# Summing the two parts of the cosines on TensorE, spacing the gate's steps, and moving second-layer parts in each stage's last unit

## The chip, the core and the metric

The kernel runs on one NeuronCore of a Trainium2 chip. The core has TensorE (PE) for matrix products, VectorE (DVE), ScalarE (ACT) and GpSimd (POOL) for work on elements, and SyncE (SP), which issues the transfers. The metric is the device time of one execution in microseconds. Before the change three executions took 1617.32, 1617.62 and 1620.14 us, so the median is 1617.62 us.

## What is computed

Three layers follow one another. The first is clustered attention: a query sees only the keys whose nearest centroid is the same as its own. The nearest centroid is the argmax of 16 cosines per row, so small errors there would change the mask. Then come a layer with softplus and a mixture whose gate is normalised eight times over rows and columns (Sinkhorn).

```python
q_assign = np.argmax(np.einsum('bhsd,hcd->bhsc', q_n, c_n), axis=-1)
k_assign = np.argmax(np.einsum('bhsd,hcd->bhsc', k_n, c_n), axis=-1)
mask = q_assign[:, :, :, None] == k_assign[:, :, None, :]
scores = np.where(mask, scale * np.matmul(q, k.transpose(0, 1, 3, 2)), -1e9)
attn = softmax(scores); x = attn @ v          # 2 x 8 heads, 768 rows, 64 wide
g = softplus(x @ w_in); x = g @ w_out         # 1536 x 512, hidden 2048
P = np.exp(x @ w_gate - max)                  # 8 experts
for _ in range(8):
    P /= P.sum(1, keepdims=True) + 1e-09
    P /= P.sum(0, keepdims=True) + 1e-09
    P *= N / E
out = sum(P[:, e:e+1] * (np.maximum(x @ w1[e], 0) @ w2[e]) for e in range(8))
```

## The kernel before, in words

**Two-part numbers.** TensorE takes float32 operands in a short format. So each operand X is split into a high part (a cast) and a low part (X minus the cast), and a product is a sum of two to four matmuls over parts.

**Attention** works on 8 pairs of heads, `g` = 0 to 7. For each pair there is preparation (loads, splits, norms, cosines, argmax, one-hot rows) and then 4 half passes of scores, exponentials, transposes and products with V. The order is written out by hand: each step is an event with a place in time (`at`, and `sched_pair`, L505 to L543); the events are sorted and issued in that order, and pair `g+1` is prepared while pair `g` is attended. The compile step may still move an instruction forward on its engine where its own model finds the engine free. Categories named in `KEEP` (L665) are pinned behind what was issued before them on their engine.

The cosines of a pair are made in two halves of 384 rows (`hf`). `pair_sims` (L428) issues four matmuls for a half: two sources (q and k) times two parts of the source, and the stationary matrix `Z` holds the centroids' high and low parts side by side. So the 128 output rows are source x head x centroid part x 16 centroids, and the two centroid parts land in different rows. ACT copies the result to `sT`. `pair_simsT` (L446) transposes it back in three TensorE transposes into the PSUM tile `tp`, ACT copies the low-part columns to `s2`, and DVE adds high-part columns and `s2` into `A`. `pair_argmax` (L459) works on `A`. The PSUM tiles `sm` and `tp` share three buffers (tag `t`) with the transposes of the exponentials (`e_trans`, L597).

**The two later layers** are one list of units (L40): 8 + 8 units of the softplus layer (kind 1, halves `sb` 0 and 1 of the rows) and 32 + 32 of the mixture (kind 2). The first 8 form their products plainly (`plain_group`, L750); the others use seven groups of matmuls per unit (`group`, L695), six matmuls of 384 columns each. Groups 1 and 3 share the PSUM bank `lb` and wait for its evacuation. A unit's second layer is cut into four parts (`layer2`, L808), which are issued between the groups of the next unit, after groups 1, 3, 5 and 6 (L989). In a stage's last unit (`final`, L965; there are four) they are not: there the inputs of the next stage are split (`x_split`, L97 and L99) after each group, and after the last group come the four parts of the unit before and the four parts of this unit.

**The gate** needs the whole softplus output. `gate(b, hf)` (L863) makes the logits of half a batch entry: four float32 matmuls into PSUM, an ACT copy `ls`, three transposes and a DVE copy into `lt`. For `b` = 0 it is called after units 2 and 3 of the second stage (L993), in the bank `lb`. For `b` = 1 it is called in the first mixture unit. The first five mixture units are held (`hold`, L950): their activations wait in `late` until the gate is done. During them a queue of 22 steps is worked off, one after each group, four in the first unit and five in each later one (L951 to L960): two gates, two steps of `gate_max` (L878), 16 steps of `sinkhorn` (L892; step 0 works on rows on DVE and leaves column sums `cs`, step 1 sums them over partitions on TensorE in `cp`, L905, and scales), then `load_p` and `spread_p`. After the fifth unit all late activations run (L1007).

Of the kernel before, what the change touches and what calls it, by code (L numbers as in the profile page):

```python
# [7 lines left out]
F32 = mybir.dt.float32  # L8
F32R = mybir.dt.float32r
# [11 lines left out]
def attention_moe_moe2(ctx, tc, q, k, v, qt, kt, centroids, w_in, w_out, w_gate, w1, w2, eye, out, dbg=None):  # L21
# [265 lines left out]
    def prep_z(c2):  # L287
        for i in range(2):
            pc = ps_m.tile([P, P], F32R, tag="t", name=f"pc{i}")
            nc.tensor.transpose(pc, c2[:, i].rearrange("p a d -> p (a d)"), idr)  # L290
            pv = pc.bitcast(F32).rearrange("p (h j c) -> p h j c", j=2, c=NC_)
            nc.vector.tensor_copy(Z0[:, :, 96 + 16 * i : 112 + 16 * i], pv[:, 0])
            for j in range(2):
                js, o = slice(j * D, (j + 1) * D), 64 + 32 * j + 16 * i
                nc.vector.tensor_copy(Z[js, :, o : o + NC_], pv[js, :, j])

# [131 lines left out]
    def pair_sims(st, hf, ph):  # L428
        g = st.g
        if ph == 0:  # L430
            if hf == 0:
                st.sT = pp.tile([P, 2, CB], F32, tag="sT", name=f"sT{g}", bufs=1)
                st.A = pp.tile([P, 2, HT * 4, NC_], F32, tag="A", name=f"A{g}", bufs=1)
            st.sm = ps_m.tile([P, CB], F32, tag="t", name=f"sm{g}{hf}")
            for n in range(4):
                w, x = divmod(n, 2)
                if g:
                    c, m = Z[:, st.hp, 64 - 64 * w : 192 - 64 * w], st.HL[w][:, x]
                else:
                    o = 64 * w + 32 * x  # L440
                    c, m = Z0[:, x, 96 - o : 224 - o], st.AT[w, x]
                nc.tensor.matmul(st.sm, c, m[:, hf * CB : (hf + 1) * CB], start=n == 0, stop=n == 3)
        else:
            nc.scalar.copy(st.sT[:, hf], st.sm)

    def pair_simsT(st, hf, ph):  # L446
        g = st.g
        if ph == 0:
            st.tp = ps_m.tile([P, HT * 4, 2, NC_], F32, tag="t", name=f"tp{g}{hf}")
            tpv = st.tp.rearrange("p (t x) a c -> p t (x a c)", t=HT)  # L450
# [54 lines left out]
    def sched_pair(g, b0):  # L505
# [26 lines left out]
        for hf in range(2):  # L532
            P_(b0 + hf + 8.27, "sm", pair_sims, hf, 0)
            P_(b0 + hf + 8.27 + .1, "smc", pair_sims, hf, 1)
            P_(b0 + 2 * hf + 11.5, "tp", pair_simsT, hf, 0)
            P_(b0 + 2 * hf + 11.5 + .1, "tpc", pair_simsT, hf, 1)
            P_(b0 + 2 * hf + 11.5 + 0.65, "tpa", pair_simsT, hf, 2)
# [127 lines left out]
    KEEP = {'sp2': 1, 'fr': 0, 'sq': 1, 'red': 1, 'av': 1, 'am3': 1, 'tpa': 1, 'smc': 0, 'm0': 1, 'nw': 0, 'nv': 1, 'rw': 1, 'pz': 1, 'e1': 1, 'ln': 0}  # L665
# [194 lines left out]
    def gtile(shape, tag, b, nm):  # L860
        return ps_y.tile(shape, F32, tag=tag, name=nm) if b else ps_l.tile(shape, F32, tag="lb", name=nm)

    def gate(b, hf):  # L863
        lg = gtile([E, CB], f"y{hf}", b, f"lg{b}{hf}")
        for c in range(KC):
            nc.tensor.matmul(
                lg, wg[:, c, :], xt[b][:, c, hf * CB : (hf + 1) * CB], start=c == 0, stop=c == KC - 1
            )
        ls = mp.tile([E, CB], F32, tag="ls", name=f"ls{b}{hf}", bufs=2)
        nc.scalar.copy(ls, lg)  # L870
        tp = gtile([P, HT, E], "y4", b, f"lgT{b}{hf}")
        for t in range(HT):
            nc.tensor.transpose(tp[:, t, :], ls[:, t * P : (t + 1) * P], idf[:E, :E])
        nc.vector.tensor_copy(lt[:, b * NT + hf * HT : b * NT + (hf + 1) * HT, :], tp)

    sm = mp.tile([P, 2], F32, tag="gm", name="gm", bufs=1)

# [59 lines left out]
    def run(*steps):  # L937
        for l in steps:
            for fn in l:
                fn()  # L940

    run(*split_unit(units[0]))
    pend = []
    starts = [n for n in range(len(units)) if n == 0 or units[n - 1][:2] != units[n][:2]]
    for n, u in enumerate(units):
# [2 lines left out]
            return  # L948
        held = n - len(m1)
        hold = 0 <= held < NHOLD  # L950
        extra = []  # L951
        if hold:
            if held == 0:
                queue = [lambda hf=hf: gate(1, hf) for hf in range(2)]
                queue += [lambda ph=ph: gate_max(ph) for ph in range(2)]
                queue += [lambda it=it, ph=ph: sinkhorn(it, ph) for it in range(8) for ph in range(2)]
                queue += [lambda: load_p(0, 0), spread_p]
            k = 4 if held == 0 else 5
            extra, queue = queue[:k], queue[k:]
        if kind == 2 and fc == 0 and not hold:  # L960
            load_p(sb, e)
        if n + 2 in starts:
# [11 lines left out]
        for i in range(7):  # L974
            if not is_plain(u):
                group(u, i)
            elif i % 2 == 0:
                plain_group(u, i // 2)
            run(steps.get(i, []))
            if n + 1 in starts:  # L980
                key = f"{units[n + 1][0]}_{units[n + 1][1]}"
                if not is_plain(u):
                    x_split(key, sums, i)
                else:
                    for c in ((4,), (5,), (0, 1), (), (), (), (2, 3, 6))[i]:
                        x_split(key, sums, c)
            if extra:
                extra.pop(0)()
            if (i % 2 == 1 or i == 6) and pend and not hold and not final:  # L989
                layer2(pend[0], i // 2)  # L990
        for fn in extra:
            fn()
        if kind == 1 and sb == 1 and 2 <= fc < 4:  # L993
            gate(0, fc - 2)
        if pend and not hold:
            p_ = pend.pop(0)
            if final:
                for part in range(4):
                    layer2(p_, part)
        pend.append(u)  # L1000
        if final:
# [1 line left out]
            for part in (0, 2, 1, 3):  # L1003
                layer2(p_, part)
        if hold and held == NHOLD - 1:
            run(queue)
            for lu, q, cols in late:  # L1007
                if (0, lu[2]) not in PB:
                    load_p(0, lu[2])
                g = GF[lu, q][:, cols]  # L1010
                nc.vector.scalar_tensor_tensor(g, g, 0.0, PB[0, lu[2]][:, cols], ALU.max, ALU.mult)
                act_split(lu, q, cols)
# [39 lines left out]
```

## Time and profile before

| | us |
|---|---|
| executions without the profiler, median of 3 | 1617.62 |
| the profiled execution, its own time | 1615.32 |
| span of its trace, first to last instruction | 1613.5 |
| PE busy (matmuls) in the span | 1536.4 (95%) |
| DVE busy | 1079.2 (67%) |
| ACT busy | 851.7 (53%) |
| POOL busy | 687.2 (43%) |

Read it from the top: the trace covers the profiled execution except for 1.8 us around it. PE's busy time is an average over stages with different limits, and matmuls overlap in the pipeline, so 95% does not say that PE is the limit everywhere. In the profile's slices DVE is at nine tenths over the first sixth of the span, which is attention, and at five to six tenths in the mixture.

### The profile page before, as it was taken

The numbers are of one execution on the slowest core, as the hardware profiler recorded it, in microseconds if no ns is written. First come the engines' busy times: TensorE is split into PE (matmuls) and PEld (weight loads), VectorE is DVE, ScalarE is ACT, GpSimd is POOL, SyncE is SP. The second block draws the span as 40 slices with busy tenths as digits, with TensorE's granted clock in tenths as the row PEclk, the third lists the DMA queues.
The fourth block names the chain that finished last, engine by engine and source line by source line (L and its number), as shares of the span: only waits on it lengthen the run. The fifth ranks groups of instructions, "written<-read, shape, count | busy, mean of one in ns | idle before, by whom it ended". The sixth has DMA issues, their size and how long they took to land.

```text
span 1613.5 us, 22747 instructions
## 1 busy us (share of the span) xinstructions
PE 1536.4 (95%) x8134; PEld 1381.5 (86%) x8134; DVE 1079.2 (67%) x1772; ACT 851.7 (53%) x1727; POOL 687.2 (43%) x681
## 2 busy tenths in 40 slices
PE   5899999888999989999999999999999999999999
PEld 4788888787897868899999999988999999999997
DVE  5999999998554768665655656577655556565553
ACT  5888988766676754343434434344434434344342
POOL 4444533334755743434434443345333343343430
PEclk8999999999999999999999999999999999999999
DMA  7666620364211221222323223223223232232211
GB/s 218 179 168 167 177 65 7 124 219 143 78 58 53 59 60 54 84 60 83 75 66 89 62 79 74 77 66 115 64 77 86 58 86 65 76 78 73 79 53 46
DMA packets 135971, 145.18 MB, mean 90 GB/s; under 512 B 9169, under 2 KB 100785, under 8 KB 135857
## 3 DMA queue, kind: packets, MB, share of 16 engines
q1 hardware_dynamic: 135712, 143.66, 31.4%
q8 instruction: 64, 1.05, 0.3%
q14 instruction: 51, 0.41, 0.1%
q10 hardware_dynamic: 144, 0.07, 0.0%
HBM read 113.23 MB, written 11.58 MB: 77 GB/s over the span
## 4 chain that ended last, share of the span: by engine, by line
PE 64%; DVE 7%; ACT 4%; issue 1%; POOL 1%; DMA 0%; DVEq 0%; ACTq 0%; POOLq 0%
PE Y L842 32%; PE la L714 16%; PE mb L714 8%; PE lb L714 4%; PE y L823 2%; DVE gf L790 1%; DVE gl L804 1%; DVE wl L226 1%; ACT gh L803 1%; ACT u L788 1%; ACT u L787 1%; PE p L767 1%; ACT u L789 1%; DVE xS L75 0%; ACT wh L225 0%
## 5 line engine op out<-in xcount | busy, mean ns | idle before, releaser
L803 ACT CAST gh<-gf 128x384 fp32r<-128x384 f32 x316 | 161.5, 513 | 479.2 <-DVE gf L797 434.5
L214 POOL TENSOR_TENSOR wf<-wf 128x256 f32<-128x256 f32 x288 | 237.3, 846 | 346.9 <-DMA wf<-in_moe_w_dram 273.7
L232 POOL TENSOR_TENSOR w2l<-w2f,w2h 128x512 fp32r<-128x512 f32 x160 | 240.3, 1522 | 314.4 <-ACT w2h L231 314.4
L842 PE MATMUL Y<-w2h,gh 128*128 128x512 f32 x768 | 299.0, 389 | 0.7 <-ACT gh L803 0.7
L842 PE MATMUL Y<-w2l,gh 128*128 128x512 f32 x768 | 298.8, 389 | 0.0
L842 PE MATMUL Y<-w2h,gl 128*128 128x512 f32 x768 | 298.5, 389 | 0.0
L804 DVE TENSOR_TENSOR gl<-gf,gh 128x384 fp32r<-128x384 f32 x316 | 207.2, 659 | 96.1 <-ACT gh L803 89.4
L741 DVE TENSOR_TENSOR gf<-la,c 128x384 f32<-128x384 f32 x71 | 39.5, 557 | 254.2 <-PE la L714 254.0
L225 ACT CAST wh<-wf 128x512 fp32r<-128x512 f32 (+1 forms) x232 | 153.0, 684 | 35.1 <-PE la L714 24.8
L842 PEld LDWEIGHTS Y<-w2h,gl 128*128 128x128 f32 x768 | 144.1, 188 | 30.1
L842 PEld LDWEIGHTS Y<-w2h,gh 128*128 128x128 f32 x768 | 144.0, 188 | 22.3 <-ACT gh L803 1.2
L842 PEld LDWEIGHTS Y<-w2l,gh 128*128 128x128 f32 x768 | 144.2, 188 | 21.0
L797 DVE SCALAR_TENSOR_TENSOR gf<-gf,pb 128x384 f32<-128x384 f32 x177 | 151.1, 854 | 4.0
L226 DVE TENSOR_TENSOR wl<-wf,wh 128x512 fp32r<-128x512 f32 (+1 forms) x194 | 151.9, 809 | 1.0 <-ACT wh L225 0.9
L608 DVE TENSOR_TENSOR el<-t,eh 128x384 fp32r<-128x384 f32 x192 | 101.5, 544 | 11.8 <-ACT eh L604 10.6
L601 PE MATMUL t<-idf,E 128*128 128x128 f32 x576 | 96.4, 276 | 8.3 <-DVE el L608 5.0
L714 PE MATMUL mb<-chS,wh 128*128 128x384 f32 x288 | 98.2, 341 | 4.3 <-DVE gf L737 4.0
L604 ACT CAST eh<-t 128x384 fp32r<-128x384 f32 x192 | 91.6, 481 | 19.3 <-PE t L601 11.6
L231 ACT CAST w2h<-w2f 128x512 fp32r<-128x512 f32 x160 | 92.3, 618 | 16.7 <-PE y L823 8.7
L714 PE MATMUL la<-chA,wh 128*128 128x384 f32 x288 | 97.8, 340 | 1.6 <-DVE gf L797 1.6
L569 DVE TENSOR_REDUCE sc<-s 128x1 f32<-128x768 f32 x96 | 91.1, 949 | 12.0 <-PE s L561 11.4
L733 ACT COPY c<-la 128x384 f32<-128x384 f32 x144 | 68.8, 478 | 57.2 <-PE la L714 55.9
(210 smaller groups left out, 3478.0 us busy)
## 6 DMA issues: line engine op xcount, KB each, us to landing
w2f<-in_moe_w_dram SPq DMA_DIRECT2D x128, 256.0 KB, 3.4
wf<-in_moe_w_dram SPq DMA_DIRECT2D x128, 256.0 KB, 3.4
AT<-HL SPq DMA_DIRECT2D x56, 192.0 KB, 4.0
r<-in_moe_w_in_dram SPq DMA_DIRECT2D x16, 512.0 KB, 5.8
r<-in_moe_w_out_dram SPq DMA_DIRECT2D x16, 512.0 KB, 5.2
pb<-pdram SPq DMA_DIRECT2D x15, 384.0 KB, 7.6
Bt<-HL SPq DMA_DIRECT2D x28, 192.0 KB, 4.1
w<-wf SPq DMA_DIRECT2D x16, 256.0 KB, 3.5
```

Of the source, the lines that this page charges most:

```text
L214: nc.gpsimd.tensor_tensor(wf[:, SLOT[o_], :], wf[:, SLOT[u_], :], wf[:, SLOT[v_], :], ALU.subtract)
L225: nc.scalar.copy(wh[:, c0:c1], wf[:, c0 + o : c1 + o, :])
L226: (nc.vector if kind == 2 or u == (1, 0, 0, 0) else nc.gpsimd).tensor_tensor(wl[:, c0:c1], wf[:, c0 + o : c1 + o, :], wh[:, c0:c1].bitcast ...
L231: nc.scalar.copy(w2h[:, c], w2f[c])
L232: nc.gpsimd.tensor_tensor(w2l[:, c], w2f[c], w2h[:, c].bitcast(F32), ALU.subtract)
L601: nc.tensor.transpose(pt[:, t * P : (t + 1) * P], Et[i, t][:, s * P : (s + 1) * P], idf)
L608: nc.vector.tensor_tensor(el, TT.pop((i, s)), EHL[i, s].bitcast(F32), ALU.subtract)
L714: nc.tensor.matmul(ps, wt[:, s_, ks], xx[:, k_, :], start=i in (0, 1, 3) and n == 0, stop=n == 3 * nk - 1, skip_group_check=True,)
L797: nc.vector.scalar_tensor_tensor(g, src, 0.0, PB[sb, e][:, cols], ALU.max, ALU.mult)
L803: nc.scalar.copy(gh[:, cols], g)
L804: nc.vector.tensor_tensor(gl[:, cols], g, gh[:, cols].bitcast(F32), ALU.subtract)
L842: nc.tensor.matmul(y[m], gt[:, ms], wt[:, q, :], start=first and i == 0, stop=last and i == 2)
```

## The change

Four edits.

1. **Cosines.** `Z` holds the two centroid parts as separate stationary matrices with 64 columns. A half takes eight matmuls instead of four, all into one PSUM tile of 64 rows, so TensorE adds the two parts. `sT` has 64 partitions, the transposes have 64 columns, ACT copies `tp` straight into `A`, and the DVE add with its event `tpa` and its place in `KEEP` is gone.
2. **Gate for `b` = 0.** `gate` has two phases: logits and `ls`; transposes and `lt`. They are called after units 2, 3, 4 and 5.
3. **Held units.** The queue is replaced by a plan of places, one for each group of the five units (35 places): logits at 0 and 1, their transposes at 2 and 3, `gate_max` at 4 and 6, step 0 of iteration `it` at 7 + 3 `it` and step 1 two places later, `load_p` at 32, `spread_p` at 33, the first four late activations at 34, the others after the unit.
4. **Last unit of a stage.** Parts 0 and 1 of the previous unit's second layer are issued after groups 1 and 3; parts 2 and 3 stay after the last group.

```diff
-    Z = pp.tile([P, NPAIR, 192], F32R, tag="Z", name="Z", bufs=1)
-    Z0 = pp.tile([P, 2, 224], F32R, tag="Z0", name="Z0", bufs=1)
+    Z = pp.tile([P, NPAIR, 2, 96], F32R, tag="Z", name="Z", bufs=1)
+    Z0 = pp.tile([P, 2, 2, 112], F32R, tag="Z0", name="Z0", bufs=1)
...
-            st.sm = ps_m.tile([P, CB], F32, tag="t", name=f"sm{g}{hf}")
-            for n in range(4):
-                w, x = divmod(n, 2)
+            st.sm = ps_m.tile([64, CB], F32, tag="t", name=f"sm{g}{hf}")
+            for n in range(8):
+                w, x, i = n // 4, n // 2 % 2, n % 2
                 if g:
-                    c, m = Z[:, st.hp, 64 - 64 * w : 192 - 64 * w], st.HL[w][:, x]
+                    c, m = Z[:, st.hp, i, 32 - 32 * w : 96 - 32 * w], st.HL[w][:, x]
...
-            st.tp = ps_m.tile([P, HT * 4, 2, NC_], F32, tag="t", name=f"tp{g}{hf}")
+            st.tp = ps_m.tile([P, HT * 4, NC_], F32, tag="t", name=f"tp{g}{hf}")
...
-                nc.tensor.transpose(tpv[:, t, :], st.sT[:, hf, t * P : (t + 1) * P], idf)
-        elif ph == 1:
-            st.s2 = pp.tile([P, HT * 4, NC_], F32, tag="s2", name=f"s2{g}{hf}", bufs=1)
-            nc.scalar.copy(st.s2, st.tp[:, :, 1, :])
-        else:
-            nc.vector.tensor_tensor(st.A[:, hf], st.tp[:, :, 0, :], st.s2, ALU.add)
+                nc.tensor.transpose(tpv[:, t, :], st.sT[:, hf, t * P : (t + 1) * P], idf[:64, :64])
+        else:
+            nc.scalar.copy(st.A[:, hf], st.tp)
...
-    def gate(b, hf):
+    def gate(b, hf, ph):
+        if ph:
+            tp = gtile([P, HT, E], "y4", b, f"lgT{b}{hf}")
+            for t in range(HT):
+                nc.tensor.transpose(tp[:, t, :], LS[b, hf][:, t * P : (t + 1) * P], idf[:E, :E])
+            nc.vector.tensor_copy(lt[:, b * NT + hf * HT : b * NT + (hf + 1) * HT, :], tp)
+            return
...
+    for hf in range(2):
+        put(hf, gate, 1, hf, 0)
+        put(2 + hf, gate, 1, hf, 1)
+        put(4 + 2 * hf, gate_max, hf)
+    for it in range(8):
+        put(7 + 3 * it, sinkhorn, it, 0)
+        put(9 + 3 * it, sinkhorn, it, 1)
...
+    put(32, load_p, 0, 0)
+    put(33, spread_p)
+    put(34, first_late)
...
-            if extra:
-                extra.pop(0)()
-            if (i % 2 == 1 or i == 6) and pend and not hold and not final:
+            if hold:
+                run(plan.get(7 * held + i, ()))
+            if (i % 2 == 1 or i == 6) and pend and not hold and (i < 4 or not final):
                 layer2(pend[0], i // 2)
-        for fn in extra:
-            fn()
-        if kind == 1 and sb == 1 and 2 <= fc < 4:
-            gate(0, fc - 2)
+        if kind == 1 and sb == 1 and 2 <= fc < 6:
+            gate(0, fc // 2 - 1, fc % 2)
         if pend and not hold:
             p_ = pend.pop(0)
             if final:
-                for part in range(4):
+                for part in range(2, 4):
                     layer2(p_, part)
```

## Rows read from the trace of the kernel before

**Rows 1.** Windows: busy us (instructions) of each engine, granted clock, DMA share, GB/s

```profile
core 0: us, PE busy (x) PEld busy (x) DVE busy (x) ACT busy (x) POOL busy (x), PEclk, DMA share, GB/s
...
40.00:275.00 235.00, 215.84 (x1400) 195.66 (x1399) 218.89 (x425) 205.22 (x459) 108.53 (x140) 0.99 0.50 131
...
604.00:641.00 37.00, 33.56 (x191) 31.37 (x190) 32.23 (x86) 14.67 (x28) 9.60 (x12) 1.00 0.19 58
...
1110.00:1613.50 503.50, 499.66 (x2499) 453.49 (x2497) 281.73 (x446) 199.09 (x380) 187.64 (x182) 1.00 0.26 73
```

**Rows 2.** Chain that ended last, mixture: start, us, what

```profile
1056.80 2.04 PE Y L842 x9
```

**Rows 3.** Groups by form, 0 to 275 us: count | busy, mean ns | idle before

```profile
L442 PE MATMUL sm<-HL,Z 128*128 128x384 f32 x56 | 13.2, 365 | 0.0
...
L452 PE MATMUL tp<-idf,sT 128*128 128x128 f32 x48 | 8.9, 294 | 0.8 <-DVE el L608 0.8
...
L457 DVE TENSOR_TENSOR A<-tp,s 128x192 f32<-128x192 f32 x16 | 5.6, 348 | 1.9 <-ACT s L455 1.9
L455 ACT COPY s<-tp 128x192 f32<-128x192 f32 x16 | 5.2, 327 | 0.8 <-ACT E L574 0.4 <-PE tp L452 0.2
```

**Rows 4.** Timeline, cosines of pair 3, first half: start, us, instruction

```profile
94.49 0.85 PE L442 MATMUL sm<-HL,Z 128*128 128x384 f32 x4
95.19 0.52 PE L561 MATMUL s<-AT,AT 128*128 128x384 f32 x2
...
99.38 0.49 PE L452 MATMUL tp<-idf,sT 128*128 128x128 f32 x3
99.62 0.60 PE L561 MATMUL s<-AT,AT 128*128 128x384 f32 x2
...
100.50 0.35 ACT L455 COPY s<-tp 128x192 f32<-128x192 f32 x1
...
103.20 0.34 DVE L457 TENSOR_TENSOR A<-tp,s 128x192 f32<-128x192 f32 x1
```

**Rows 5.** Waits, 40 to 275 us: us in total, times, longest us

```profile
DVE el L608 <- ACT eh L604: 9.2, 24, 0.9
...
PE t L601 <- DVE el L608: 4.7, 9, 1.0
...
DVE sc L569 <- PE s L561: 3.2, 9, 0.9
```

**Rows 6.** Timeline of PE at the start of the kernel

```profile
12.14 2.30 PE L442 MATMUL sm<-AT,Z 128*128 128x384 f32 x8
14.31 0.55 PE L452 MATMUL tp<-idf,sT 128*128 128x128 f32 x3
...
24.55 2.85 PE L442 MATMUL sm<-HL,Z 128*128 128x384 f32 x8
28.29 0.95 PE L561 MATMUL s<-Bt,Bt 80*128 80x384 f32 x4 [0.89 <-DMA Bt<-OHT]
```

**Rows 7.** Windows, as Rows 1, the start of pair 0's scores

```profile
24.00:28.00 4.00, 3.40 (x14) 2.91 (x14) 0.01 (x1) 0.85 (x2) 0.80 (x2) 0.59 0.63 184
```

**Rows 8.** Timeline of PE after unit 2 of the second stage

```profile
490.85 0.35 PE L873 MATMUL lgT<-idf,ls 8*128 8x8 f32 x3 [1.12 <-ACT ls L870]
...
492.29 0.44 PE L714 MATMUL lb<-chA,wh 128*128 128x384 f32 x1 [0.32 <-DVE lt L874]
```

**Rows 9.** Waits, held units, 604 to 641 us

```profile
PE cp L905 <- DVE cs L901: 3.1, 3, 1.1
```

**Rows 10.** Line L897 (a small DVE step of the gate): ns min/median/max, first and last start

```profile
L897 DVE TENSOR_SCALAR rs<-rs x8: 173/174/716, 602.7 to 637.7; 128x12 f32<-128x12 f32 x8
```

**Rows 11.** Timeline of PE in the last units of stages 1, 2 and 3

```profile
426.68 0.44 PE L767 MATMUL p<-chA,wh 128*128 128x384 f32 x1 [1.83 <-DVE gf L790]
...
584.15 0.62 PE L823 MATMUL y<-gl,w2h 128*128 128x512 f32 x2 [1.99 <-DVE gl L804]
...
1089.58 0.45 PE L714 MATMUL mb<-chS,wh 128*128 128x384 f32 x1 [1.77 <-DVE gf L737]
```

**Rows 12.** Windows, as Rows 1, last units of stages 2 and 3

```profile
569.70:584.20 14.50, 11.07 (x61) 8.98 (x59) 13.19 (x13) 10.94 (x22) 11.62 (x8) 1.00 0.20 53
...
1084.20:1094.30 10.10, 8.13 (x44) 7.39 (x44) 10.03 (x11) 6.99 (x12) 7.37 (x5) 1.00 0.37 105
```

More of the change, by code (lines that the diff above doesn't have):

```diff
@@ L291, in prep_z @@
             pv = pc.bitcast(F32).rearrange("p (h j c) -> p h j c", j=2, c=NC_)
-            nc.vector.tensor_copy(Z0[:, :, 96 + 16 * i : 112 + 16 * i], pv[:, 0])
+            nc.vector.tensor_copy(Z0[:, :, i, 48:64], pv[:, 0])
             for j in range(2):
-                js, o = slice(j * D, (j + 1) * D), 64 + 32 * j + 16 * i
-                nc.vector.tensor_copy(Z[js, :, o : o + NC_], pv[js, :, j])
+                js, o = slice(j * D, (j + 1) * D), 32 + NC_ * j
+                nc.vector.tensor_copy(Z[js, :, i, o : o + NC_], pv[js, :, j])
     def last_of_engines(engines):
@@ L431, in pair_sims @@
             if hf == 0:
-                st.sT = pp.tile([P, 2, CB], F32, tag="sT", name=f"sT{g}", bufs=1)
+                st.sT = pp.tile([64, 2, CB], F32, tag="sT", name=f"sT{g}", bufs=1)
                 st.A = pp.tile([P, 2, HT * 4, NC_], F32, tag="A", name=f"A{g}", bufs=1)
-            st.sm = ps_m.tile([P, CB], F32, tag="t", name=f"sm{g}{hf}")
-            for n in range(4):
-                w, x = divmod(n, 2)
+            st.sm = ps_m.tile([64, CB], F32, tag="t", name=f"sm{g}{hf}")
+            for n in range(8):
+                w, x, i = n // 4, n // 2 % 2, n % 2
                 if g:
-                    c, m = Z[:, st.hp, 64 - 64 * w : 192 - 64 * w], st.HL[w][:, x]
+                    c, m = Z[:, st.hp, i, 32 - 32 * w : 96 - 32 * w], st.HL[w][:, x]
                 else:
-                    o = 64 * w + 32 * x
-                    c, m = Z0[:, x, 96 - o : 224 - o], st.AT[w, x]
-                nc.tensor.matmul(st.sm, c, m[:, hf * CB : (hf + 1) * CB], start=n == 0, stop=n == 3)
+                    o = 32 * w + 16 * x
+                    c, m = Z0[:, x, i, 48 - o : 112 - o], st.AT[w, x]
+                nc.tensor.matmul(st.sm, c, m[:, hf * CB : (hf + 1) * CB], start=n == 0, stop=n == 7)
         else:
@@ L861, in gtile @@
         return ps_y.tile(shape, F32, tag=tag, name=nm) if b else ps_l.tile(shape, F32, tag="lb", name=nm)
-    def gate(b, hf):
+    LS = {}
+    def gate(b, hf, ph):
[5 more added lines that the diff above has]
+            return
         lg = gtile([E, CB], f"y{hf}", b, f"lg{b}{hf}")
@@ L868, in gate @@
             )
-        ls = mp.tile([E, CB], F32, tag="ls", name=f"ls{b}{hf}", bufs=2)
+        ls = LS[b, hf] = mp.tile([E, CB], F32, tag="ls", name=f"ls{b}{hf}", bufs=2)
         nc.scalar.copy(ls, lg)
[L871 to L874, printed above, removed]
     sm = mp.tile([P, 2], F32, tag="gm", name="gm", bufs=1)
@@ L940, in run, with put, late_acts, first_late @@
                 fn()
+    plan = {}
+    def put(place, fn, *args):
+        plan.setdefault(place, []).append(lambda: fn(*args))
+    for hf in range(2):
[5 more added lines that the diff above has]
+        put(9 + 3 * it, sinkhorn, it, 1)
+    def late_acts(pieces):
+        for lu, q, cols in pieces:
+            if (0, lu[2]) not in PB:
+                load_p(0, lu[2])
+            g = GF[lu, q][:, cols]
+            nc.vector.scalar_tensor_tensor(g, g, 0.0, PB[0, lu[2]][:, cols], ALU.max, ALU.mult)
+            act_split(lu, q, cols)
+    def first_late():
+        late_acts(late[:4])
+        del late[:4]
+    put(32, load_p, 0, 0)
+    put(33, spread_p)
+    put(34, first_late)
+    assert 34 == 7 * NHOLD - 1
     run(*split_unit(units[0]))
@@ L950, in attention_moe_moe2 @@
         hold = 0 <= held < NHOLD
[L951 to L959, printed above, removed]
         if kind == 2 and fc == 0 and not hold:
@@ L1005, in attention_moe_moe2 @@
         if hold and held == NHOLD - 1:
[L1006 to L1012, printed above, removed]
+            late_acts(late)
             while len(pend) > 1:
```

5 lines of the change are left out of this document (2 added, 3 removed).

## The prediction

> **What bounds the kernel now.** I read the busy time by stage first, then the chain that ended last, then the waits inside each stage the change touches. The stages have different limits. From 40 to 275 us, attention, DVE is busy for 218.89 of 235 us and PE's matmuls for 215.84, so neither has much room and DVE is the fuller [rows 1]. What idle time DVE has, 16.1 us, is mostly waits for tiles that PE feeds: 9.2 us for `eh` and 3.2 us for scores [rows 5]. From 1110 us to the end PE is busy for 499.66 of 503.5 us [rows 1]: that is a solid stream, in which a part of the second layer, nine matmuls, takes 2.04 us [rows 2]. Nothing in the change shortens that stream. So the change can only win in attention, or where PE now stands still: in the gate for `b` = 0, in the held units (3.4 us idle of 37.0, [rows 1]) and in the last unit of each stage.
>
> **Cosines in attention.** Removed: 16 DVE adds of 348 ns [rows 3]. Four of them lie before 40 us, so the steady part loses 12 x 0.348 = 4.2 us of DVE time. ACT's 16 copies of 327 ns [rows 3] stay; only their target changes. Added: 64 matmuls of 384 columns, 48 of them after 40 us. The four now issued for a half start at 94.49 and the next matmul at 95.19, which is 0.175 us each [rows 4], so 48 cost 8.4 us of PE's issue time. Each has 64 stationary columns instead of 128; I take no saving for that. The three transposes of a half take 99.62 - 99.38 = 0.24 us [rows 4]; with half the columns they could save half, 12 x 0.12 = 1.4 us, or nothing. So PE gets 7.0 to 8.4 us more work and DVE 4.2 us less.
>
> Which of the two counts? PE's matmul rows leave 235 - 215.84 = 19.2 us idle, and its weight loads, 195.66 us, leave 39 us [rows 1]. DVE's ready work is the narrower, so I count its 4.2 us in full and let a fifth of PE's 8.4 us, 1.7 us, reach DVE as later `eh` and scores; the fifth is my estimate, between none and all of it. That gives **-2.5 us**. Bounds: the tile `tp` now holds one of three PSUM buffers from 99.38 until the add ends at 103.54, and in the new order only until the ACT copy ends at 100.85 [rows 4]. At most this ends the 4.7 us that PE waits for `el` before transposes [rows 5], so the low end is -4.2 - 4.7 = -8.9; the high end, with all of PE's work on the path and none of DVE's saving, is +8.4.
>
> A rule speaks to the same choice. The Trainium skill, Perfetto Trace Analysis, section Identifying the Most-Contended Engine, says that matmul busy share is a poor measure for TensorE, that weight-load share is a better one, and that occupancy is fair for VectorE. Read by that rule PE has 17% to spare here against DVE's 7%, and the sum would be the full -4.2 us; read by the matmul rows the two are even and the gain could be used up.
>
> **The start.** Pair 0's and pair 1's cosines run while PE is slow: eight matmuls take from 12.14 to 14.31, 0.27 us each, and the next eight span 2.85 us, 0.36 us each [rows 6]. In the second stretch the granted clock is 0.59, near the lower level of 1.2 GHz, after PE had idled [rows 7]. Eight more for pair 0 cost up to 2.2 us on the way to its argmax, less two adds, 0.7 us. Eight more for pair 1 cost up to 2.9 us ahead of the first masked scores, less the 0.89 us that PE waits there for a transfer anyway [rows 6]. At most 1.5 + 2.0 = +3.5; at least -0.7, if other work covers both. I take the middle, **+1.5 us**. Attention in all: -1.0.
>
> **Gate for b = 0.** PE now waits 1.12 us for `ls` and 0.32 us for bank `lb` [rows 8]; the second gate waits for next to nothing. With the transposes a unit later `ls` is long there. But `lb` is taken four times instead of twice, so a wait of 0.3 us may come back twice. **-1.2 us**, bounds -1.6 and +0.6.
>
> **Held units.** The first of the 16 steps starts at the same place as before, the last `sinkhorn` step moves from place 28 to 30, `load_p` from 29 to 32. PE waits for `cs` for 3.1 us, in three places of 1.0 to 1.1 us, one a unit [rows 9]. With two groups of PE work between the steps of an iteration, most of this should go. What is late next is DVE: it is busy for 32.23 of 37.0 us [rows 1], and without PE's waits the stretch would be 33.6 us, so DVE would have 4% left. So I take two thirds, **-2.0 us**; bounds -3.4 (all PE idle time) and +3.2 (the chain really ends three places later, three groups of 6 x 0.175 us, and the late activations wait for it). `first_late` is issued directly ahead of the rest of the same list, so it costs and gives nothing; the transfer of `spread_p` moves three places on SP and is needed only by the fifth unit's activations, tens of us of second layer later.
>
> **Last units.** Stage 1: PE waits 1.83 us for an evacuation behind DVE's input splits [rows 11]; a part moved up gives PE 2 us of work there and four parts remain for the own unit's activations to hide behind. -1.8, bounds -1.8 and 0. Stage 3: the wait of 1.77 us has the same cause [rows 11]; the moved parts end it, but this unit's activations come later against two parts less of cover, with DVE full (10.03 of 10.10, [rows 12]). -1.5, bounds -1.8 and +1. Stage 2: the wait of 1.99 us stands *after* the groups, for the own unit's `gl` [rows 11], while DVE is busy for 13.19 of 14.50 us [rows 12]. There DVE sets the end, and parts moved ahead of it only lengthen the wait behind them. 0, bounds -2 and +2. Last stage: no splits, no waits, the same matmuls: 0. Together **-3.3 us**.
>
> **Sum.** -1.0 - 1.2 - 2.0 - 3.3 = -7.5 us. Against the profiled execution's own 1615.32 us (span 1613.5, 1.8 us around it) that is 1607.8. The median of the runs, 1617.62, stands 2.3 us above that execution, so the forecast is 1610.0 us. About 0.2%, 3.2 us, is what a measurement of this kernel can tell from no change.
>
> **Rivals.**
> *A. The held units' waits have another cause.* L897 takes 174 ns in the median and up to 716 ns [rows 10]: small DVE steps are sometimes stretched fourfold, and then `cs` is late wherever the steps stand. The places were already overtaken by the data. Against it: only three waits reach 1 us. The held units then give 0: 1612.0 us. The Trainium skill, SBUF — State Buffer, section Who interferes with whom, has a rule for such stretching: GpSimd and VectorE share a port pair, and whichever starts first keeps it for the whole instruction. By that rule the waits would follow GpSimd's sums of weights, one set a unit, and spacing would not end them; three waits over three units agree with it, but no row here shows the lock itself.
> *B. The cosines' matmuls use up what the add gave.* If half of PE's 8.4 us reaches the path and the start costs its 3.5, attention is -4.2 + 4.2 + 3.5 = +3.5, and with the other terms, -6.5, and a waiting second stage, +2, the time is 1616.6: no change that can be told. For it: PE's matmul rows are as full as DVE's.
> *C. Slower.* One mechanism: PE, not DVE, sets attention's pace. Then 64 matmuls are on the path, 48 x 0.175 + 3.5 = +11.9 with nothing back from DVE; with -6.5 elsewhere it is +5.4, 1623.0 us. It decides if DVE's waits for `eh` and scores, 12.4 us now, grow by more than about 10 us. Against it: DVE has the least idle time of all engines there.
>
> **Chances.** Forecast 0.50, A 0.20, B 0.20, C 0.10. Forecast and A are faster by over 0.2%, B is within it, C slower: 0.70, 0.20, 0.10. The range runs from 1602 (attention near its low bound, -8.9, or every wait gone) to 1619, above B; C and a little below are left out.
>
> **What would show it.** In attention: DVE's busy time from 40 to 275 us down by about 4 us, the stretch 2 to 3 us shorter, and PE's waits for `el` smaller; wrong if DVE's waits for `eh` and scores grow. At the start: the first masked scores, now at 28.29, at 29 to 31. `lgT` without a wait. In the held units `cp` waits under 1 us in all; rival A if three waits of 1 us remain. In the last units of stages 1 and 3 no wait over 1 us; in stage 2 a longer one for `gl`. The stream from 1110 us on must keep its length; if it does not, the cause is outside this working.

## The result, and the profile after

The changed kernel is slower by 1.1%: 1636.39 us (median of 4 runs, 1631.87 to 1637.4) against 1618.82 us (4 runs) for the kernel before on the same chip, a ratio of 1.0108, 95% interval 1.0095 to 1.012. The forecast was 1610.0. The profiled execution of the changed kernel took 1637.4 us, 22.1 us more than that of before; that is more than the medians' 17.6 us, since it is the slowest of its four runs, and that of before is faster than all four of its own. Its span is 1635.6 us. Placed by the starts of the same instructions in the two traces, the difference lies here:

| from | to | before, us | after, us | difference |
|---|---|---|---|---|
| start | first product with `v` | 37.9 | 38.9 | +1.0 |
| there | last product with `v` | 250.2 | 264.1 | +13.9 |
| there | end of `y`, `b` = 0 (stage 1) | 158.2 | 155.9 | -2.3 |
| there | end of `y`, `b` = 1 (stage 2, with the gate of `b` = 0) | 143.9 | 141.1 | -2.8 |
| there | first `Y` (held units) | 55.6 | 59.6 | +4.0 |
| there | middle of the `Y` matmuls (stage 3) | 473.6 | 481.6 | +8.0 |
| there | end | 494.2 | 494.4 | +0.2 |

Three notes on reading it. The two groups of matmuls that before stood behind the first `Y`, 11 matmuls or some 2 us, stand ahead of it after, so about 2 us of the held units' +4.0 belong to stage 3. Seven traces with the attention code of before, that of the kernel before and six below, end attention at 287.4 to 289.7 us; their first product with `v` starts at 36.4 to 37.9 us, and from first to last it takes 250.0 to 251.8 us, so a difference under 2 us in one trace says little there. And eleven traces whose code behind attention is that of before take 529.0 to 532.6 us from the end of `y` to the middle of the `Y` matmuls (529.2 before, 541.2 after), so there a single trace tells nothing below some 4 us.

**Attention.** Windows of the changed kernel (attention, the held units, the last stream), columns as in [rows 1]:

```profile
core 0: us, PE busy (x) PEld busy (x) DVE busy (x) ACT busy (x) POOL busy (x), PEclk, DMA share, GB/s
40.00:289.60 249.60, 228.39 (x1453) 200.25 (x1452) 222.23 (x413) 207.49 (x460) 107.40 (x139) 0.99 0.47 124
613.90:654.90 41.00, 37.44 (x202) 33.14 (x202) 32.61 (x92) 16.85 (x33) 13.62 (x16) 1.00 0.18 52
1131.90:1635.60 503.70, 499.86 (x2499) 453.49 (x2497) 287.85 (x446) 198.75 (x380) 189.33 (x182) 1.00 0.26 72
```

What was 40 to 275 us takes 14.6 us longer. PE is busy for 12.6 us more, of which the 48 added matmuls are 8.4 us, and DVE, which lost 12 adds there, is busy for 3.3 us more. From 0 to the end of attention, where both traces hold the same work but for the cosines, DVE is busy for 253.60 us after and 253.88 before, though 16 adds, 5.6 us, are gone. The last row is the stream from 1110 us of before: 503.70 against 503.5, as it was.

The waits of DVE and PE from 40 to 289.6 us (us in total, times, longest us):

```profile
DVE sc L565 <- PE s L557: 12.0, 18, 1.4
DVE el L604 <- ACT eh L600: 10.6, 22, 1.1
DVE mx L469 <- POOL A L466: 2.5, 4, 0.7
...
PE t L597 <- DVE el L604: 6.6, 16, 0.8
```

Against [rows 5] DVE waits for scores for 12.0 us instead of 3.2. PE's wait for `el`, which a shorter hold of `tp` was to end, grew from 4.7 to 6.6. The 2.5 us that the argmax waits for GpSimd's step on `A` are not among DVE's waits before. A half's cosines on PE, pair 4 (start, us, instruction), and the ones at the start:

```profile
24.46 4.62 PE L442 MATMUL sm<-HL,Z 128*64 128x384 f32 x16
28.93 0.86 PE L557 MATMUL s<-Bt,Bt 80*128 80x384 f32 x4
...
133.97 1.55 PE L442 MATMUL sm<-HL,Z 128*64 128x384 f32 x8
135.36 0.51 PE L557 MATMUL s<-AT,AT 128*128 128x384 f32 x2
```

Eight matmuls hold PE from 133.97 to 135.36, 0.174 us each, as four did [rows 4]; half the stationary columns save nothing. The first masked scores stand at 28.93 instead of 28.29 [rows 6], without the wait for a transfer; but TensorE's first instruction of all already stands at 8.39 instead of 7.67.

**Last units.** PE's waits there, timeline of the changed kernel (stage 1's last unit has none left):

```profile
588.66 0.39 PE L819 MATMUL y<-gl,w2h 128*128 128x256 f32 x1 [1.19 <-DVE gl L800]
591.34 1.22 PE L819 MATMUL y<-gh,w2h 128*128 128x512 f32 x2 [1.22 <-ACT gh L799]
1114.97 0.44 PE L710 MATMUL la<-chA,wh 128*128 128x384 f32 x1 [0.92 <-DVE gf L737]
1122.87 0.50 PE L838 MATMUL Y<-w2h,gl 128*128 128x512 f32 x1 [2.02 <-DVE gl L800]
1124.41 0.63 PE L838 MATMUL Y<-w2l,gh 128*128 128x512 f32 x1
1124.84 0.63 PE L838 MATMUL Y<-w2h,gl 128*128 128x512 f32 x1
```

The 1.83 us of stage 1 [rows 11] are gone. In stage 3 the 1.77 us for `gf` are gone, and in their place PE waits 2.02 us for the unit's own `gl`; from 1123.98 on the next matmuls start 0.43 us apart instead of 0.23.

**Held units and the stage behind them.** PE's waits from 601 to 659.6 us:

```profile
PE la L710 <- ACT c L729: 1.4, 3, 0.6
PE mb L710 <- DVE gf L733: 1.0, 2, 0.7
PE cp L905 <- DVE cs L901: 0.7, 1, 0.7
PE mb L710 <- DVE gfx L733: 0.6, 1, 0.6
PE pb L924 <- DVE Pt L908: 0.5, 1, 0.5
```

The waits of `cp`, 3.1 us in [rows 9], are down to 0.7, and 3.5 us of others are new. Then comes something that no step of the prediction had. Timelines of PE, POOL and SP's transfers of the changed kernel:

```profile
679.91 0.69 PE L838 MATMUL Y<-w2l,gh 128*128 128x512 f32 x1 [3.30 <-POOL w2l L232]
...
661.79 15.32 POOL L214 TENSOR_TENSOR wf<-wf 128x256 f32<-128x256 f32 x4 [6.28 <-DVE gl L800]
677.06 4.04 POOL L232 TENSOR_TENSOR w2l<-w2f,w2h 128x512 fp32r<-128x512 f32 x3
...
658.44 0.42 SPq L190 DMA_DIRECT2D wf<-in_moe_w_dram  x1
660.34 0.37 SPq L934 DMA_DIRECT2D pb<-pdram  x1
```

and of POOL and SP in the kernel before, in the same place:

```profile
655.19 6.27 POOL L232 TENSOR_TENSOR w2l<-w2f,w2h 128x512 fp32r<-128x512 f32 x2 [10.48 <-ACT w2h L231]
...
669.87 3.63 POOL L214 TENSOR_TENSOR wf<-wf 128x256 f32<-128x256 f32 x4 [3.20 <-DMA wf<-in_moe_w_dram]
...
645.22 0.38 SPq L934 DMA_DIRECT2D pb<-pdram  x1
...
665.55 0.93 SPq L190 DMA_DIRECT2D wf<-in_moe_w_dram  x2
```

Before, a unit's weights were fetched behind the transfer of `pb`, and behind `w2f`; their four sums on POOL then came after `w2l`. Now `spread_p` comes three places later, the weights' transfer stands ahead of `pb` on SP, the sums are ready early, and on POOL they go ahead of `w2l`. They take 15.32 us instead of 3.63, and PE waits 3.30 us for `w2l`. That the order on SP brought about the one on POOL is read from these lines; no run tests it.

### The profile page after: what moved, and what is told of

It reads as the page before. It is cut to its first block, busy times and chain, and to the rows that moved or that the text cites. A ratio compares the mean times of both kernels' runs of the same rounds, so it can differ in the third digit from the quotient of the medians.

```text
span 1635.6 us, 22856 instructions
## 1 busy us (share of the span) xinstructions
PE 1560.2 (95%) x8198; PEld 1391.4 (85%) x8198; DVE 1073.4 (66%) x1756; ACT 853.9 (52%) x1727; POOL 692.8 (42%) x681
## 4 chain that ended last, share of the span: by engine, by line
PE 64%; DVE 6%; ACT 3%; POOL 2%; issue 1%; DMA 1%; DVEq 0%; SPq 0%; ACTq 0%; POOLq 0%
PE Y L838 30%; PE la L710 16%; PE mb L710 8%; PE lb L710 4%; PE y L819 3%; POOL wf L214 1%; DVE gl L800 1%; PE p L763 1%; DVE gf L786 1%; ACT u L784 1%; ACT u L783 1%; ACT gh L799 1%; DVE xS L75 1%; ACT u L785 0%; DVE gf L793 0%
## 5 line engine op out<-in xcount | busy, mean ns | idle before, releaser
L214 POOL TENSOR_TENSOR wf<-wf 128x256 f32<-128x256 f32 x288 | 247.7, 881 | 366.5 <-DMA wf<-in_moe_w_dram 288.8
L232 POOL TENSOR_TENSOR w2l<-w2f,w2h 128x512 fp32r<-128x512 f32 x160 | 235.6, 1491 | 304.4 <-ACT w2h L231 304.4
L838 PE MATMUL Y<-w2h,gh 128*128 128x512 f32 x768 | 300.5, 391 | 0.1
L710 PE MATMUL la<-chS,wh 128*128 128x384 f32 x288 | 97.9, 340 | 1.4 <-ACT c L729 1.4
```

The costliest lines, as they stand in the source:

```text
L214: nc.gpsimd.tensor_tensor(wf[:, SLOT[o_], :], wf[:, SLOT[u_], :], wf[:, SLOT[v_], :], ALU.subtract)
L232: nc.gpsimd.tensor_tensor(w2l[:, c], w2f[c], w2h[:, c].bitcast(F32), ALU.subtract)
L710: nc.tensor.matmul(ps, wt[:, s_, ks], xx[:, k_, :], start=i in (0, 1, 3) and n == 0, stop=n == 3 * nk - 1, skip_group_check=True,)
L838: nc.tensor.matmul(y[m], gt[:, ms], wt[:, q, :], start=first and i == 0, stop=last and i == 2)
```

## The experiments

Whole times are medians of the runs; a ratio is to the kernel before on the same chip. The kernels of experiments 2 to 5 ran once each. "Attention ends" is the start of the last product with `v`, 288.1 us before and 303.0 after.

**1. The cosines apart from the rest.** `rest` is the changed kernel with the old cosines, `cos` the kernel before with the new cosines alone.

> The changed kernel with the cosines of the kernel before: wide products in four matmuls, the add on VectorE with its pin; the gate's order, the held units' plan and the last units stay changed. Theory 'cosines': attention ends where it did before, its last product with v near 288 us (before 288.1, after 303.0), and the whole is about 15 us below the changed kernel, 1621 to 1623 us by the median, still slower than before by the held units and the first mixture stage (+4.0 and +7.6 us in the traces, less 5 us that the two earlier stages gained). Rival 'the traces only differ': attention stays near 303 and the whole near 1636.

> The kernel before with the cosines' part of the change alone. Theory 'cosines': last product with v near 303 us, whole near 1632 to 1634 us (before plus 15). If the loss needs the other parts too, below 1625.

`rest`: 1624.32 us, 1.3 us above the range, ratio 1.0042 (1.0024 to 1.0059), attention ends at 287.8. `cos`: 1632.75 us, ratio 1.0076 (1.0052 to 1.0101), attention ends at 303.7. So the cosines alone make attention's whole loss, some 12 us by the ratio and 15.6 by the traces, and the other parts together lose 0.42%.

**2. TensorE's work, or the order?** Three edits of the kernel before: each matmul doubled with a zero stationary half (`dbl`); the new cosines without the low part (`hi`); the pin of the add taken off (`nopin`). The lines of `hi` are set against the changed kernel.

```
 dbl:  nc.tensor.matmul(st.sm, c, mm, start=n == 0, stop=False, ...)
      +nc.tensor.matmul(st.sm[0:64], Z0[:, x, 0:64], mm, start=False, stop=n == 3, ...)
 hi:  -for n in range(8):  w, x, i = n // 4, n // 2 % 2, n % 2
      +for n in range(4):  w, x, i = n // 2, n % 2, 0
 nopin: KEEP without 'tpa': 1
```

> The kernel before with each of the cosines' four matmuls followed by a second of the same moving columns whose stationary half is zero, so TensorE does the eight matmuls of the changed kernel (0.70 us more for each half of a pair, 11 us in all), while VectorE keeps its add, its pin and all its other work. Theory 'work of TensorE': the changed kernel's loss comes from the eight matmuls standing in front of the scores, so attention ends at 299 to 306 us and the whole is 1630 to 1637 us (VectorE keeps 4 us more than in the changed kernel). Rival 'pin': the loss comes from the order that the add's pin had held, so attention ends within 3 us of 288 and the whole near 1618 to 1621 us.

> The kernel before with the changed kernel's cosines, but of the centroids' high part alone: four matmuls for each half as before, no low part (the cosines leave the centroids' low part out), and no add and no pin on VectorE. Theory 'work of TensorE': with the work of TensorE as before and 4 us less on VectorE attention ends at 283 to 289 us, whole 1613 to 1620 us. Rival 'pin': the order is the changed kernel's, attention ends at 299 to 304 us, whole 1630 to 1634 us.

> The kernel before with nothing changed but the pin on VectorE's add of the cosines, which is taken off: same work on every engine, only what the pin held in order may move. Theory 'work of TensorE': attention ends within 2 us of 288.1, whole 1615 to 1620 us. Rival 'pin' (it carries the 3 us of the changed kernel's loss that the doubled matmuls left unexplained, or more): attention ends at 291 us or later, whole 1621 us or more.

`dbl`: attention ends at 299.1 us, +11.0; the whole, 1628.05, is 2 us below the range. 64 more matmuls at 0.174 us are 11.1 us, but that this agrees with 11.0 is in part luck: the whole +11.0 lies between first and last product with `v` (261.2 us; 250.0 to 251.8 in the seven traces), where 48 of the 64 stand, 8.4 us. So TensorE's added work came through at its full length and somewhat more, 9.4 to 11.2 us. DVE's waits in `dbl`, 40 to 286 us:

```profile
DVE sc L571 <- PE s L563: 11.3, 15, 2.2
DVE el L610 <- ACT eh L606: 11.1, 24, 1.1
```

They are the changed kernel's waits, without its other edits. `nopin`: 290.7 us, between the two ranges and 1.0 us above the latest of the seven traces, whole 1618.91, so the pin carries a small part at most. `hi` was a miss for both theories: 292.7 us, whole 1621.12. It has TensorE's old work and 5.6 us less on VectorE, and is no faster. Of its +4.6 us 3.1 lie ahead of the first product with `v` (40.9 us), where PE waits 2.93 us for a transfer instead of 0.89 [rows 6]:

```profile
30.57 1.62 PE L557 MATMUL s<-Bt,Bt 80*128 80x384 f32 x4 [2.93 <-DMA Bt<-OHT]
```

From first to last product it takes 251.8 us, as the slowest of the seven. So between the products VectorE's saving gave nothing. The next views say where it went.

**Where VectorE's saving went.** Groups of DVE by form: the mask in the argmax (line L473 before, L470 in the changed kernel and in `hi`), from 0 to the end of attention, before:

```profile
L473 DVE TENSOR_TENSOR A<-A,mx 128x384 f32<-128x384 f32 x8 | 5.6, 695 | 0.0
```

in `hi`:

```profile
L470 DVE TENSOR_TENSOR A<-A,mx 128x384 f32<-128x384 f32 x8 | 10.2, 1276 | 0.1
```

and one of them, with what POOL does, in the changed kernel's timeline:

```profile
44.77 2.17 DVE L470 TENSOR_TENSOR A<-A,mx 128x384 f32<-128x384 f32 x1
...
44.69 1.83 POOL L366 TENSOR_TENSOR HL<-rT,HL 128x768 fp32r<-128x768 f32 x1
```

Alone this instruction takes 0.55 us. Here it starts 0.08 us after POOL's split of the next pair and ends 0.42 us after it, 2.17 us in all. In `hi` seven of the eight overlap that split, and the group costs 4.6 us more, which is most of the 5.6 us of adds. In the changed kernel the mask (+1.7), the conversions of weights into `w2f` (+1.7) and the step of `sc` (+1.3) grew; the instructions that grew there overlap one on POOL too. So DVE's busy time to the end of attention is 253.62 us in `hi` and 253.60 in the changed kernel, against 253.88 before: the saving did not arrive. The Trainium skill, SBUF — State Buffer, section Who interferes with whom, says that a VectorE instruction with two SBUF inputs contends with a GpSimd instruction that reads SBUF; these rows agree.

**3. The burst.** From pair 1 on `split` puts the eight matmuls of a half into two bursts of four, a step apart.

```
-P_(b0 + hf + 8.27, "sm", pair_sims, hf, 0)
+P_(b0 + 2 * hf + 8.27, "sm", pair_sims, hf, 0, 0)
+P_(b0 + 2 * hf + 9.27, "sm", pair_sims, hf, 0, 1)
```

> The kernel before with the changed kernel's cosines, but from pair 1 on the eight matmuls of a half stand in two bursts of four, a step (some 1.35 us) apart, so that no burst in front of the scores is longer than before. Theory 'length of the burst' (what costs is that the scores' next product waits behind 1.4 us of matmuls): attention ends at 288 to 294 us, whole 1618 to 1624 us. Rival 'sum of TensorE's work' (each matmul more costs its 0.175 us wherever it stands): 299 to 304 us, whole 1629 to 1634 us.

Attention ends at 302.5 us, whole 1633.44, both as the rival has it: a shorter burst gives nothing back.

**4. Less work on TensorE.** `cut` issues two of a half's four matmuls:

```
-for n in range(4):
+for n in (0, 2):
```

> The kernel before with two of the four cosine matmuls of a half left out (the low parts of q and k are left out of the cosines), 0.35 us of TensorE less for each half, 5.6 us in all; VectorE and ScalarE as before. Theory 'each matmul counts, both ways': attention ends at 281 to 285 us. Rival 'threshold' (TensorE only sets the pace when more is added; before, VectorE and ScalarE set it): 286 to 290 us.

Attention ends at 288.2 us, whole 1615.32: 5.6 us less of TensorE's work, 4.2 of them between the products with `v` (251.1 us), gave nothing. DVE's waits from 40 to 290 us, before:

```profile
DVE el L608 <- ACT eh L604: 10.6, 27, 0.9
DVE sc L569 <- PE s L561: 3.2, 9, 0.9
```

and in `cut`:

```profile
DVE el L608 <- ACT eh L604: 14.1, 34, 0.9
DVE sc L569 <- PE s L561: 2.0, 6, 0.6
```

The waits for scores shrank and the waits for `eh` grew. So TensorE alone does not bound attention before, and yet what is added to it counts. One run says so, and its instructions stand in another order on TensorE too.

**5. One order for all.** In experiments 2 to 4 the compiler also placed the scores, transposes and products in another order in each kernel. Pins on those events hold one order on TensorE in four kernels; in their traces it is the same in all four.

```
-if cat and cat[0] in KEEP and cat[1] >= KEEP[cat[0]]:
+if cat and (... or cat[0] in ('s0', 's1', 's2', 'e0', 'e1', 'e2', 'av', 'sm', 'tp')):
```

> The kernel before with the attention's scores, transposes, products with v and cosines pinned to the order in which the program names them. The base for the three below, not a better kernel: attention end anywhere from 286 to 305 us. Its distance from 288.1 is what an order alone can do; near 288 an order is worth little, and 15 us later an order alone could make the change's loss.

> The same pins with the changed kernel's cosines: eight matmuls, no add on VectorE. Theory 'work of TensorE': attention ends 9 to 15 us after the pinned kernel with the old cosines. Rival 'order': within 3 us of it.

> The same pins with the changed kernel's cosines but four matmuls (the centroids' low part is left out of the cosines), no add on VectorE. If VectorE's 4.2 us less are worth their price when nothing else moves: 3 to 5 us before the pinned kernel with the old cosines. If VectorE's work alone does not set the pace: within 1.5 us of it.

> The same pins with the old cosines and each of their matmuls doubled, VectorE as before. Theory 'work of TensorE': 9 to 15 us after the pinned kernel with the old cosines, and 0 to 4 us after the pinned one with the new cosines. Rival 'order': within 3 us of the first.

Attention ends at 328.2, 346.0, 341.8 and 339.8 us (old cosines, new, new without the low part, doubled). Of the ranges only the first for the doubled cosines holds; the base itself lies 23 us above its own. The ends differ by the start too: in the doubled one TensorE begins 2.2 us later. From first to last product with `v` they take 291.6, 308.0, 302.1 and 299.8 us. So doubling costs 8.2 us in one and the same order, about the length of its 48 added matmuls (8.4 at 0.174 us each), and the low part's matmuls in the new cosines cost 5.9. But the old cosines lose 40 us by the pins alone, which is more than the change does, the new cosines without the low part lose 10.4 us with no more work on TensorE, and the granted clock of these stretches differs (0.93 with the old cosines, 0.91 with the new, 0.99 without the pins). So these four bear out the price of the added matmuls, and show that an order or the new cosines' form can cost as much. Of the changed kernel's 12.3 to 14.1 us between the products (264.1 against the seven traces) the matmuls' own length is 8.4; whether the other 4 to 6 us are its order, its missing pin, the new wait for GpSimd's `A` or something else stays open.

**6. The parts that work.** `g_l` is the kernel before with the gate of `b` = 0 in two steps and the last units' edit alone; in `best` the last units' edit is kept to the stages of layer 1:

```
-... and not hold and (i < 4 or not final):
+... and not hold and (i < 4 and kind == 1 or not final):
...
-    for part in range(2, 4):
+    for part in range(2 if kind == 1 else 0, 4):
```

> The kernel before with the gate of b=0 in two steps and the parts of a second layer in the last units, and neither the new cosines nor the new plan of the held units. If these two give what the traces of the changed kernel show (2.3 us in stage 1 with b=0, 2.8 us in stage 1 with b=1, held units and mixture as before): 1611 to 1614 us, faster by 0.2 to 0.4 per cent. Rival 'their gain is given back in the held units': 1616 to 1619 us.

> The kernel before with the gate of b=0 in two steps, and with the parts of a second layer in the last unit in the two stages of layer 1 alone; the mixture's last units keep the order of before. Theory 'in the mixture the parts had covered the unit's own activations': the wait for gl of 2.2 us and the slow matmuls behind it near 1099 us go, the wait of 1.9 us near 1090 us comes back, and the whole is 2 to 4 us below the run with both (1614.4): 1610 to 1613 us, faster than before by 0.35 to 0.5 per cent. Rival: 1614 us or more.

`g_l`: 1614.38 us, ratio 0.9977 (0.9964 to 0.999), at the upper edge of its range. `best`: 1613.47 us, ratio 0.9976 (0.9966 to 0.9985), the lowest median of the study, 0.5 us above its range. From the end of `y` to the middle of the `Y` matmuls `g_l` takes 532.6 us and `best` 530.1, against 529.2 before. PE's waits at its end, `g_l`:

```profile
1099.19 0.50 PE L842 MATMUL Y<-w2h,gl 128*128 128x512 f32 x1 [2.02 <-DVE gl L804]
```

and `best`:

```profile
1086.66 0.44 PE L714 MATMUL mb<-chS,wh 128*128 128x384 f32 x1 [1.79 <-DVE gf L737]
```

The wait for `gl` and the one for `gf` exchange as expected. But of 2 to 4 us nothing shows: the medians differ by 0.9 us, the runs of before beside them by as much, so the ratios are the same; and 532.6 us is no more than one of the eleven traces with the order of before takes. That the edit costs anything in the mixture is not shown.

**7. GpSimd's queue.** The sums of one unit are made to issue behind `w2l` of an earlier one, in `rest`: first those of the first unit behind the held ones (`rest_pool`), then those of the third (`rest_pool2`).

```
 def sums_():
+    if u == units[len(m1) + NHOLD + 2]:     # rest_pool: + NHOLD
+        for ins in W2L[units[len(m1) + 3]]: es.enter_context(tc.issue_after(ins))
```

> The run before with the old cosines and all other parts of the change, with one order more: GpSimd's four weight sums for the first unit behind the held ones issue only after its low part of w2 of the fourth held unit, as they stood in the kernel before. Theory 'GpSimd's queue': the wait for w2l of 3.3 us in the first mixture stage and the slow matmuls behind it go, so first Y to first output shrinks by 4 to 7 us and the whole is 1616 to 1620 us. Rival 'VectorE's stream slows whatever GpSimd does there': the wait for w2l stays over 2 us and the whole is within 2 us of the run without it (1624).

> As the run with the old cosines and all other parts, but the one order added is on the sums that the trace shows ahead of w2l: those of the third unit behind the held ones issue after the low part of w2 of the fourth held unit, so GpSimd's sums and low parts of w2 stand in the order of the kernel before. (The pin before sat on the first unit behind the held ones, and the wait moved to the next unit's w2l, 3.7 us.) Theory 'GpSimd's queue': no wait for w2l over 1 us between 640 and 700 us, whole 1613 to 1618 us, at or below the kernel before; what is left of the mixture's loss, some 3 us, is the last unit's. Rival: the wait moves once more, whole 1620 us or more.

`rest_pool`: 1622.13 us, above its range, ratio 1.0028 (1.0015 to 1.0042). I had put the pin on the wrong unit, and the wait moved:

```profile
678.99 0.80 PE L852 MATMUL Y<-w2l,gh 128*128 128x512 f32 x1 [3.74 <-POOL w2l L241]
```

`rest_pool2`: 1616.31 us, ratio 0.9992 (0.9982 to 1.0002), 8 us below `rest`. Timelines of POOL and SP's transfers there:

```profile
654.39 7.67 POOL L241 TENSOR_TENSOR w2l<-w2f,w2h 128x512 fp32r<-128x512 f32 x2 [13.51 <-ACT w2h L240]
...
665.24 3.77 POOL L216 TENSOR_TENSOR wf<-wf 128x256 f32<-128x256 f32 x4
...
643.82 0.43 SPq L190 DMA_DIRECT2D wf<-in_moe_w_dram  x1
645.94 0.37 SPq L948 DMA_DIRECT2D pb<-pdram  x1
```

The sums are back behind `w2l` and take 3.77 us, and stage 3's loss falls from 7.9 to 1.1 us, while on SP the weights still stand ahead of `pb`. So the order on SP costs nothing by itself here; the one on GpSimd's queue, with nothing added or removed, is worth half a per cent.

**8. Is the held units' plan worth anything?** `best2` is `best` with the plan and with that order.

> The same with the held units' new plan too, and the order on GpSimd's sums that keeps them behind w2l. If the held units then give the 2 us forecast (the waits of cp gone, nothing behind w2l): 1608 to 1611 us. Rival 'the new waits take their place' (for c, gf and Pt, 4.2 us in the changed kernel): 1611 to 1615 us, no better than without the plan.

1614.61 us, ratio 0.9981 (0.997 to 0.9991), against `best`'s 1613.47. PE's waits in the held units, up to first `Y`, in `best`:

```profile
PE cp L909 <- DVE cs L905: 3.0, 3, 1.1
```

and in `best2`:

```profile
PE mb L724 <- DVE gf L747: 1.8, 2, 0.9
PE mb L724 <- DVE gfx L747: 0.7, 1, 0.7
PE la L724 <- ACT c L743: 0.6, 1, 0.6
PE pb L938 <- DVE Pt L922: 0.6, 1, 0.6
```

3.0 us of waits for `cs` went and 3.7 us of others came. The intervals overlap: the plan gives nothing that the runs can tell.

## Why the prediction was wrong

- **The cosines: the step "I count its 4.2 us in full and let a fifth of PE's 8.4 us, 1.7 us, reach DVE" failed in both halves.** All of PE's work came through: doubling the 48 matmuls, 8.4 us, cost 8.2 us in one and the same order and 9.4 to 11.2 us without the pins. And of DVE's saving almost nothing remained (253.88 to 253.60 us busy), since other VectorE steps met POOL and grew. The choice went by which engine is fuller. `cut` says that "Which of the two counts?" was the wrong question: taking work from TensorE gave nothing, adding some cost its full length. DVE is at 93%, PE at 92% and ACT at 87% of 235 us [rows 1]; that they wait for each other in turn, so that a saving on one is taken up by the others and a burden is not, fits the waits of `cut` and is argued, not shown. With -2.5 expected and 12 to 14 measured, this step alone turns the sum's sign. The rule of the Trainium skill weighed there (Perfetto Trace Analysis, Identifying the Most-Contended Engine), that weight-load share is the better measure for TensorE, gave it 17% to spare; the added matmuls found none of it.
- **The high bound, +8.4, was too low.** It priced the matmuls alone; between first and last product with `v` the change costs 12.3 to 14.1 us, and the cause of what is above 8.4 is open.
- **The start** came out at +1.0 for +1.5, with masked scores at 28.93 where 29 to 31 was named. That is luck in part: 0.7 of it stands ahead of TensorE's first instruction, and the seven traces alone differ by 1.5 us there.
- **Rival C came nearest**, with a chance of 0.10, and its test was the right one: it "decides if DVE's waits for `eh` and scores, 12.4 us now, grow by more than about 10 us". They are 22.6 us. But only half of its mechanism held, since `cut` does not show PE setting the pace before, and its 1623.0 us is 13 us short. "Against it: DVE has the least idle time of all engines there" was true and no argument.
- **Gate for `b` = 0 and stage 2's last unit**: -1.2 and 0 forecast, -2.8 in the trace for both. **Stage 1's last unit**: -1.8 forecast, -2.3 in the trace. Both stages together take 297.0 to 298.7 us in the seven traces with these edits and 300.5 to 303.0 in seven without them and without pins. In `best` these three give -3.9 us by the ratio, which is the part of the change that works.
- **Stage 3's last unit**: -1.5 forecast. The named wait went, and a wait for the own `gl` took its place, as the prediction had foreseen for stage 2 and priced at +1 at most here. So the gain did not come; whether there is a loss, the traces and runs of `g_l` and `best` can't tell.
- **Held units: two steps failed.** "Most of this should go" holds for `cp` (3.1 to 0.7 us), but "what is late next is DVE" was priced at a third of the gain, and it took all of it. And "the transfer of `spread_p` moves three places on SP and is needed only by the fifth unit's activations" asked who needs the transfer, not what it is moved past: a unit's weights overtook it on SP, their sums overtook `w2l` on POOL, and the order on POOL cost 8 us.
- **The stream from 1110 us** kept its length, 503.70 for 503.5.

Between the sum, -7.5, and the traces, +22.1, lie 29.6 us: 16.4 are the cosines, and 15.5 lie between the end of `y` and the middle of the `Y` matmuls (-3.5 forecast, +12.0 in the traces). Of these 15.5 the order on POOL is 8; the rest is the gain of 3.5 us that did not come, and 4 us, hardly more than the 3.6 us by which traces of the same code differ there. The start, the gate and the last units of stages 1 and 2 came out 2.6 us better.

## What to carry to other kernels

Where several engines stand within some per cent of full and feed each other, price added work on any of them in full and a saving on one of them at nothing, until one run with work added and one with work taken away show which is which. For a step that is moved, list what it now stands behind and what now stands ahead of it on every queue, SP's and GpSimd's too: here work that went ahead of a needed step on GpSimd cost more than the move could give. A part of the next layer that fills a wait also covered something behind it; moving it up can pay only where the unit's own activations are not the next to be late.

## What was not expected of the hardware

The first of GpSimd's four sums in the 15.32 us at 661.79, 0.74 us in the median, took 12.75 us. It ended at 674.5. Up to 673.9 DVE ran the late activations one behind the other, each with two inputs from SBUF; then came the first with an input from PSUM (`lb`):

```profile
672.93 1.01 DVE L800 TENSOR_TENSOR gl<-gf,gh 128x384 fp32r<-128x384 f32 x2
673.87 0.54 DVE L733 TENSOR_TENSOR gf<-lb,c 128x384 f32<-128x384 f32 x1
674.45 0.56 DVE L793 SCALAR_TENSOR_TENSOR gf<-gf,pb 128x384 f32<-128x384 f32 x1
```

In `rest` the same sum took 12.61 us and ended in the same way. So a run of more than twenty short VectorE instructions held GpSimd off as one long instruction would, as far as spans on POOL can be trusted. At 44.77 us it was VectorE that was held, by one GpSimd instruction. The Trainium skill, SBUF — State Buffer, section Who interferes with whom, speaks of a lock that is held for a whole instruction. In these two traces GpSimd got no turn between VectorE's instructions either.

After PE's wait of 3.30 us the granted clock was 0.51, near the lower level of 1.2 GHz, where it had been 1.00:

```profile
670.00:676.00 6.00, 6.00 (x29) 4.95 (x27) 4.97 (x11) 1.20 (x3) 6.00 (x3) 1.00 0.01 3
680.00:683.40 3.40, 3.40 (x9) 2.62 (x10) 0.92 (x1) 1.03 (x2) 2.37 (x2) 0.51 0.58 184
```

These are windows of the changed kernel around that wait. Eight matmuls at 0.43 instead of 0.23 us add 1.6 us to the wait. After the wait of 2.02 us at 1122.87 the same happened, and eight slow matmuls added 1.5 us. So these two waits cost half to three quarters as much again as they show. After the 1.77 us of the kernel before [rows 11] it did not happen; after the 1.79 us of `best` it did, with a granted clock of 0.51.
